# Attention block with a key and value cache: transposing key loads with rows of 16 keys in place of 4

## The chip, the cores and the metric

The kernel runs on one core of one Trainium2 chip. The metric is the device time of one launch in microseconds (us). The engines are named as in the profile: PE (matrix engine; PEld is its weight load), DVE (vector engine), ACT (scalar engine), POOL (general purpose) and SP (which here only issues DMA transfers and waits).

## The reference

The reference is a multi-head attention whose keys and values come from a cache, between an input and an output projection. Everything is bf16.

```
B, Sq, D = 8, 112, 640          H, Sk, Dh = 32, 512, 192
q = (x @ wq), split into H heads of Dh
scores = q . k_cache  * Dh**-0.5          # per batch and head: 112 x 512
p = softmax(scores)
o = p @ v_cache
out = o (heads joined) @ wo               # 8 x 112 x 640
```

The inputs are `x` (8 x 112 x 640), `k_cache` and `v_cache` (8 x 32 x 512 x 192, 50.3 MB each), `wq` (640 x 6144) and `wo` (6144 x 640).

## The kernel before

**Tiling.** The 32 heads are cut into 4 groups of 8 (`HG`, `NHG`). A unit `u` is one batch with one group of 8 heads, so there are 32 units. A turn `t` is a pair of batches, 16 in all, and a step `n` is one half unit, 4 heads, 64 in all; a turn has four steps. `place(n)` gives turn, unit, batch and half of a step.

**Order of the work.** Every piece of work is entered in a plan (`Plan.add`) with its engine, the pieces it depends on, and the function that emits it. The order on each engine is written out by hand near the end (the lists `pe`, `act`, `dve`; SP's list is filled by the load functions). Semaphore waits are worked out from the dependences. An engine works through its list in order, so a piece that waits holds up everything behind it.

**One step** is: query copies (`qc`, DVE), 16 score matmuls on PE (`scores`: L270 and L272 over 128 rows, then L282 and L284 over 64 rows in pairs), for each head a pass that scales and takes the maximum (L297, DVE) and an exp (L302, ACT) that also gives the row sum, then the reciprocal (L314) and the normalisation (L306) on DVE. One step later, PE transposes p (L322), ACT and DVE copy it out (L328), and again one step later PE multiplies with the values (L344, L355) and ACT copies the result out (L363). Between these stand pieces of the query projection for later turns (L224, copied out by L230) and of the output projection for earlier turns (L378). In ACT's list the order in a step is exp 0, exp 1, the copy L363 of two steps back, exp 2, query copies, exp 3, the copy L328 of the step before. The transposes of PE depend on L363.

**Key loads.** `load_k` (L112 to L119) reads a unit's keys with a transposing DMA on SP's queue. The source is seen as rows of 4 keys (`q=4`): 8 heads x 128 rows, each 4 x 192 = 768 elements or 1,536 B. The transposition puts each group of 128 columns of a row on the 128 partitions, so the tile `kt` is `[128, 2, 3, 1024]`: 6 groups of 128 columns, written `(a m)`, and 1,024 rows. Two neighbouring keys fill three groups: `m = 0` has the first 128 elements of the even key, `m = 2` the last 128 of the odd key, `m = 1` the remaining 64 of each. There are three such buffers (`NB = 3`); a load waits until both halves of the unit three before have had their score matmuls (`kd`). The first two units are loaded in halves of 4 heads.

**Value loads.** `load_v` (L121 to L127) reads the values without transposition; partition r holds keys 4r to 4r+3 of each head. The score columns of a head therefore come out in four blocks of 128: even and odd keys (`e`, two PSUM banks), in each `a = 0, 1`, and in a block the row r. So block `(e, a)` of p is transposed to one row per partition r, and `QJ = [0, 2, 1, 3]` names the key of the group of 4 that belongs to it.

**SP's queue** holds, from turn 2 on, for each turn: the two key loads, sometimes two `wq` loads, the two value loads, sometimes two `wo` loads. All transfers, with x at the start and the results at the end, go through it in that order.

Of the kernel before, what the change touches and what calls it, by code (L numbers as in the profile page):

```python
# [5 lines left out]
BF16 = mybir.dt.bfloat16  # L6
F32 = mybir.dt.float32
ACTF = mybir.ActivationFunctionType
# [44 lines left out]
def build_mha_kernel(nc, x, k_cache, v_cache, wq, wo, out):  # L53
    B, SQ, D = x.shape
# [9 lines left out]
    scale = float(DH) ** -0.5  # L64
    NB, NSS = 3, 3
    QJ = [0, 2, 1, 3]

    def place(n):

# [11 lines left out]
    with ExitStack() as es:  # L81
# [170 lines left out]

        def scores(n):
            t, u, b, half = place(n)
            ktb = kt[u % NB]
            xs = slice((b % 2) * SQ, (b % 2 + 1) * SQ)

            def raw(j, c):
                return qr[:, t % 2, 2 * half + j, c, xs]

            def cs(i):
                return slice((4 * half + i) * 128, (4 * half + i + 1) * 128)

            for j in range(2):
                def emit(e, j=j):
                    for h in range(2):
                        i = 2 * j + h
                        ev, od = (raw(j, 0), qh[:, n % 2, j, 1, :]) if h == 0 else (qh[:, n % 2, j, 2, :], raw(j, 2))
                        hs = slice(h * 256, (h + 1) * 256)
                        e.matmul(ps[0:SQ, 2 * j, hs], ev, ktb[:, :, 0, cs(i)], start=(h == 0), stop=False,  # L270
                                 skip_group_check=True)
                        mm = e.matmul(ps[0:SQ, 2 * j + 1, hs], od, ktb[:, :, 2, cs(i)], start=(h == 0), stop=False,  # L272
                                      skip_group_check=True)
                    return mm
                add("PE", ("Sm", n, j), [("qc", n), k_of(n), ("smax", n - 1, 2 * j), ("smax", n - 1, 2 * j + 1)], emit)
            for i in range(4):
                def emit(e, i=i):
                    j, h = divmod(i, 2)
                    ev, od = ((raw(j, 1)[0:64], qh[64:128, n % 2, j, 0, :]) if h == 0 else
                              (qh[0:64, n % 2, j, 3, :], raw(j, 1)[64:128]))  # L280
                    hs = slice(h * 256, (h + 1) * 256)
                    m1 = e.matmul(ps[0:SQ, 2 * j, hs], ev, ktb[0:64, :, 1, cs(i)], start=False, stop=True,  # L282
                                  skip_group_check=True)
                    m2 = e.matmul(ps[0:SQ, 2 * j + 1, hs], od, ktb[64:128, :, 1, cs(i)], start=False, stop=True,  # L284
                                  skip_group_check=True)
                    return m1, m2
                add("PE", ("St", n, i), [], emit, ("PE", "PE2"))

        def softmax(n):
            for i in range(4):  # L290
# [8 lines left out]
                                           op0=ALU.mult, op1=ALU.min, accum_out=nmx[:, k:k + 1])  # L299

                def exp(e, k=k, a=a):
                    return e.activation(p_sb[:, k, :], s_sb[:, a, :], ACTF.Exp, bias=nmx[:, k:k + 1], scale=-1.0,  # L302
                                        accum_out=rsum[:, k:k + 1])

                def norm(e, k=k):
# [310 lines left out]
```

## Time and profile before

| | |
|---|---|
| time, 3 runs | median 478.77 us (475.12 to 479.36) |
| profiled execution | 477.02 us, span in the profile 475.2 us |
| mean granted PE clock | 0.986 |
| busy | PE 434.7, PEld 392.8, DVE 360.9, ACT 330.3 us |
| score matmuls L270, L272, L282, L284 | 16 a step, 274 to 296 ns mean by form |
| exp L302 | 256 of 112 x 512, 712 ns mean, and 189 ns each for reading the sum |
| key loads L117 | 34 issues, 10.3 us median from issue to landing |
| value loads L125 | 30 of 1,536 KB, 10.3 us, and 4 of half the size, 6.0 us |
| DMA | 119.62 MB, 252 GB/s over the span |

An instruction's line is its line in the kernel. A mean of one instruction on PE includes its passage through the array; matmuls follow each other more closely than that. "Busy" is the time in which an engine had at least one instruction at work. Idle time of an engine that bounds nothing costs nothing. Step times quoted later run from the first score matmul of one step to that of the next.

### The profile page before, as it was taken

The numbers are of one execution on the slowest core, as the hardware profiler recorded it, in microseconds if no ns is written. First come the engines' busy times: TensorE is split into PE (matmuls) and PEld (weight loads), VectorE is DVE, ScalarE is ACT, GpSimd is POOL, SyncE is SP. The second block draws the span as 40 slices with busy tenths as digits, with TensorE's granted clock in tenths as the row PEclk, the third lists the DMA queues.
The fourth block names the chain that finished last, engine by engine and source line by source line (L and its number), as shares of the span: only waits on it lengthen the run. The fifth ranks groups of instructions, "written<-read, shape, count | busy, mean of one in ns | idle before, by whom it ended". The sixth has DMA issues, their size and how long they took to land.

```text
span 475.2 us, 14596 instructions
## 1 busy us (share of the span) xinstructions
PE 434.7 (91%) x6116; PEld 392.8 (83%) x6116; DVE 360.9 (76%) x1153; ACT 330.3 (70%) x778; POOL 0.7 (0%) x6
## 2 busy tenths in 40 slices
PE   3588669999999999999999799989989999999986
PEld 3477559999978888898999789879978989989876
DVE  0576748889878887888888688878968888888771
ACT  2376736778757775886778578767857877677673
POOL 0000000000000000000000000000000000000000
PEclk9799979999999999999999999999999999999999
DMA  8999999999999999999999999999999999999201
GB/s 184 294 269 218 311 260 239 347 217 329 282 287 249 251 324 205 329 213 310 268 225 307 221 341 195 283 265 219 326 228 342 189 295 235 315 223 321 90 17 46
DMA packets 253569, 119.62 MB, mean 252 GB/s; under 512 B 203456, under 2 KB 253504, under 8 KB 253504
## 3 DMA queue, kind: packets, MB, share of 16 engines
q1 hardware_dynamic: 253504, 118.70, 106.5%
q8 instruction: 48, 0.79, 0.7%
q14 instruction: 17, 0.14, 0.1%
HBM read 66.06 MB, written 1.15 MB: 141 GB/s over the span
## 4 chain that ended last, share of the span: by engine, by line
PE 65%; DMA 23%; SPq 6%; ACT 3%; issue 1%; DVE 1%; DVEq 0%
DMA kt<-in_k_cache_dram 18%; PE ps L378 14%; PE ps L224 12%; PE ps L355 9%; PE ps L322 8%; PE ps L282 6%; PE ps L344 5%; PE ps L270 5%; DMA vt<-in_v_cache_dram 5%; PE ps L272 4%; SPq L117 4%; ACT p_sb L302 2%; SPq L131 1%; PE ps L410 1%; ACT oT_sb L363 1%
## 5 line engine op out<-in xcount | busy, mean ns | idle before, releaser
L302 ACT ACTIVATE p_sb<-s_sb,nmx 112x512 bf16<-112x512 f32 x256 | 182.3, 712 | 117.0 <-DVE s_sb L297 117.0
L297 DVE TENSOR_SCALAR_CACHE_REDUCE s_sb<-ps 112x512 f32<-112x512 f32 x256 | 161.6, 687 | 59.1 <-PE ps L284 59.1
L224 PE MATMUL ps<-xT_sb,wq_sb 128*128 128x224 bf16 x960 | 115.4, 265 | 8.7 <-DMA wq_sb<-in_wq_dram 7.2
L378 PE MATMUL ps<-oT_sb,wo_sb 128*128 128x224 bf16 x900 | 105.0, 259 | 1.0 <-ACT oT_sb L363 1.0
L224 PEld LDWEIGHTS ps<-xT_sb,wq_sb 128*128 128x128 bf16 x960 | 91.2, 100 | 11.4 <-issue 7.2
L378 PEld LDWEIGHTS ps<-oT_sb,wo_sb 128*128 128x128 bf16 x900 | 83.7, 98 | 1.1 <-ACT oT_sb L363 1.1
L306 DVE TENSOR_SCALAR p_sb<-p_sb,rinv 112x512 bf16<-112x512 bf16 x256 | 78.9, 350 | 4.6
L230 ACT ACTIVATE qr<-ps 128x448 bf16<-128x448 f32 (+1 forms) x128 | 55.6, 439 | 16.4 <-PE ps L224 16.3
L322 PE MATMUL ps<-ident,p_sb 112*128 112x112 bf16 x1024 | 61.3, 213 | 2.8 <-ACT oT_sb L363 2.7
L322 PEld LDWEIGHTS ps<-ident,p_sb 112*128 112x128 bf16 x1024 | 53.3, 98 | 10.3 <-ACT oT_sb L363 10.3
L355 PE MATMUL ps<-pT_sb,vt 128*128 128x112 bf16 x1024 | 61.5, 213 | 0.0
L328 ACT ACTIVATE pT_sb<-ps 128x896 bf16<-128x896 bf16 x64 | 57.7, 902 | 1.6 <-PE ps L322 1.6
L355 PEld LDWEIGHTS ps<-pT_sb,vt 128*128 128x128 bf16 x1024 | 51.4, 98 | 5.0
L270 PE MATMUL ps<-kt,qr 128*112 128x256 bf16 x128 | 35.8, 279 | 20.6 <-DMA kt<-in_k_cache_dram 12.9
L328 DVE COPY pT_sb<-ps 128x896 bf16<-128x896 bf16 x64 | 40.0, 624 | 13.3 <-PE ps L322 12.9
L302 ACT ACTIVATION_READ_ACCUMULATOR p_sb<-s_sb,nmx 112x1 f32 x256 | 48.3, 189 | 0.0
L363 ACT ACTIVATE oT_sb<-ps 128x672 bf16<-128x672 f32 x64 | 45.3, 708 | 3.0 <-PE ps L355 3.0
L344 PE MATMUL ps<-pT_sb,vt 128*64 128x112 bf16 x1024 | 37.4, 216 | 3.3 <-ACT p_sb L302 1.6
L344 PEld LDWEIGHTS ps<-pT_sb,vt 128*64 128x64 bf16 x1024 | 28.1, 110 | 15.0 <-issue 11.8
L270 PEld LDWEIGHTS ps<-kt,qr 128*112 128x112 bf16 x128 | 16.8, 132 | 23.3 <-issue 10.3
L270 PE MATMUL ps<-kt,qh 128*112 128x256 bf16 x128 | 35.5, 277 | 0.0
L272 PE MATMUL ps<-kt,qh 128*112 128x256 bf16 x128 | 35.5, 277 | 0.0
(35 smaller groups left out, 424.9 us busy)
## 6 DMA issues: line engine op xcount, KB each, us to landing
vt<-in_v_cache_dram SPq DMA_DIRECT2D x30, 1536.0 KB, 10.3
wq_sb<-in_wq_dram SPq DMA_DIRECT2D x16, 480.0 KB, 5.2
wo_sb<-in_wo_dram SPq DMA_DIRECT2D x16, 480.0 KB, 12.6
vt<-in_v_cache_dram SPq DMA_DIRECT2D x4, 768.0 KB, 6.0
out_dram<-o_out SPq DMA_DIRECT2D x8, 140.0 KB, 1.9
kt<-in_k_cache_dram SPq DMA_TRANSPOSE x34, 10.3
xT_sb<-in_x_dram SPq DMA_TRANSPOSE x3, 6.2
```

The lines of the kernel that those rows point to most:

```text
L224: mm = e.matmul(ps[:, bank, j * S2:(j + 1) * S2], wq_sb[:, hg % 2, dc, c0:c0 + 128], xT_sb[:, dc, bp * S2:(bp + 1) * S2], start=(dc == 0), ...
L230: return e.activation(qr[:, t % 2, lp, blocks[0]:blocks[0] + n, :], ps[:, bank, 0:n * S2].rearrange("p (c s) -> p c s", c=n), ACTF.Copy)
L270: e.matmul(ps[0:SQ, 2 * j, hs], ev, ktb[:, :, 0, cs(i)], start=(h == 0), stop=False, skip_group_check=True)
L272: mm = e.matmul(ps[0:SQ, 2 * j + 1, hs], od, ktb[:, :, 2, cs(i)], start=(h == 0), stop=False, skip_group_check=True)
L297: return e.tensor_scalar(s_sb[:, a, :].rearrange("p (e c) -> p e c", e=2), ps[0:SQ, 2 * j:2 * j + 2, h * 256:(h + 1) * 256], -scale, None, ...
L302: return e.activation(p_sb[:, k, :], s_sb[:, a, :], ACTF.Exp, bias=nmx[:, k:k + 1], scale=-1.0, accum_out=rsum[:, k:k + 1])
L306: return e.tensor_scalar(p_sb[:, k, :], p_sb[:, k, :], rinv[:, k:k + 1], None, op0=ALU.mult)
L322: mm = e.transpose(psb[:, 4 + j, c:c + SQ], p_sb[:, (4 * n + 2 * j + h) % 8, q * 128:(q + 1) * 128], ident[0:SQ, 0:SQ])
L328: return e.activation(dst, src, ACTF.Copy) if j == 0 else e.tensor_copy(dst, src)
L344: mm = e.matmul(ps[64 * h:64 * h + 64, 4 + j, SQ:2 * SQ], vtb[:, 4 * half + 2 * j + h, d0:d0 + 64], pT(j, h, q), start=(q == 0), stop=(q = ...
L355: mm = e.matmul(ps[:, 4 + j, 2 * h * SQ:(2 * h + 1) * SQ], vtb[:, 4 * half + 2 * j + h, d0:d0 + 128], pT(j, h, q), start=(q == 0), stop=(q ...
L378: mm = e.matmul(ps[:, 7, j * S2:(j + 1) * S2], wo_sb[:, hg % 2, k, m * 128:(m + 1) * 128], oT_sb[:, t % 2, k, :], start=(k == 0), stop=(k ...
```

## The change

The source of a key load is seen as rows of 16 keys (`KQ = 16`): 8 heads x 32 rows (`KR = 32`), each 3,072 elements or 6,144 B, so 24 groups of 128 columns (`NC`). The tile `kt` has the same size but the shape `[128, 24, 256]`, with the groups written `(k a m)`: k = 0 to 3, then a and m as before. Key number 16r + 4k + 2a + e stands in row r, r = 0 to 31.

A score matmul still has 256 columns, but reads them as `a` (2), `k` (4), 32 rows: 8 runs of 32 columns, where there were 2 runs of 128. The scores of one block `(e, a)` therefore come out in the order k, r. The value rows want position 4r + k, since key 16r + 4k + 2a + e lies in value row 4r + k. The exp reads its 512 elements in the order in which they stand and writes each to that position: within a block of 128, 32 elements 4 apart, four times over. The pass that scales and takes the maximum, the normalisation, the transposes, the value matmuls, the value loads, the order of the queues and all dependences are as before.

```diff
+    KQ = 16
+    KR = SK // KQ
+    NC = KQ * DH // 128
...
-        kt = [sb(f"kt{j}", [128, 2, 3, HG * 128], BF16) for j in range(NB)]
+        kt = [sb(f"kt{j}", [128, NC, HG * KR], BF16) for j in range(NB)]
...
-                src = k_cache[b, hg * HG + lo:hg * HG + hi].rearrange("u (r q) d -> (u r) (q d)", q=4)
-                dst = kt[u % NB][:].rearrange("p a m c -> p (a m) c")[:, :, lo * 128:hi * 128]
+                src = k_cache[b, hg * HG + lo:hg * HG + hi].rearrange("u (r q) d -> (u r) (q d)", q=KQ)
+                dst = kt[u % NB][:, :, lo * KR:hi * KR]
                 return e.dma_start_transpose(dst, src)
...
-            ktb = kt[u % NB]
+            ktb = kt[u % NB][:].rearrange("p (k a m) c -> p a k m c", a=2, m=3)
...
-                return slice((4 * half + i) * 128, (4 * half + i + 1) * 128)
+                return slice((4 * half + i) * KR, (4 * half + i + 1) * KR)
...
-                        e.matmul(ps[0:SQ, 2 * j, hs], ev, ktb[:, :, 0, cs(i)], start=(h == 0), stop=False,
+                        e.matmul(ps[0:SQ, 2 * j, hs], ev, ktb[:, :, :, 0, cs(i)], start=(h == 0), stop=False,
...
-                    m1 = e.matmul(ps[0:SQ, 2 * j, hs], ev, ktb[0:64, :, 1, cs(i)], start=False, stop=True,
+                    m1 = e.matmul(ps[0:SQ, 2 * j, hs], ev, ktb[0:64, :, :, 1, cs(i)], start=False, stop=True,
...
-                    return e.activation(p_sb[:, k, :], s_sb[:, a, :], ACTF.Exp, bias=nmx[:, k:k + 1], scale=-1.0,
+                    dst = p_sb[:, k, :].rearrange("p (j r k) -> p j k r", j=4, r=KR)
+                    src = s_sb[:, a, :].rearrange("p (j k r) -> p j k r", j=4, r=KR)
+                    return e.activation(dst, src, ACTF.Exp, bias=nmx[:, k:k + 1], scale=-1.0,
                                         accum_out=rsum[:, k:k + 1])
```

The other two score matmuls (L272, L284) change in the same way.

More of the change, by code (lines that the diff above doesn't have):

```diff
@@ L269, in emit @@
                         hs = slice(h * 256, (h + 1) * 256)
[L270 removed]
+                        e.matmul(ps[0:SQ, 2 * j, hs], ev, ktb[:, :, :, 0, cs(i)], start=(h == 0), stop=False,
                                  skip_group_check=True)
[L272 removed]
+                        mm = e.matmul(ps[0:SQ, 2 * j + 1, hs], od, ktb[:, :, :, 2, cs(i)], start=(h == 0), stop=False,
                                       skip_group_check=True)
@@ L281, in emit @@
                     hs = slice(h * 256, (h + 1) * 256)
-                    m1 = e.matmul(ps[0:SQ, 2 * j, hs], ev, ktb[0:64, :, 1, cs(i)], start=False, stop=True,
+                    m1 = e.matmul(ps[0:SQ, 2 * j, hs], ev, ktb[0:64, :, :, 1, cs(i)], start=False, stop=True,
                                   skip_group_check=True)
-                    m2 = e.matmul(ps[0:SQ, 2 * j + 1, hs], od, ktb[64:128, :, 1, cs(i)], start=False, stop=True,
+                    m2 = e.matmul(ps[0:SQ, 2 * j + 1, hs], od, ktb[64:128, :, :, 1, cs(i)], start=False, stop=True,
                                   skip_group_check=True)
```

## The prediction

> **What bounds the kernel now.** I read the page's busy shares and the chain that ended last first, then how long a step takes in the stretches, then the packets of the DMA queue, then the order of instructions within one step.
>
> ```profile
> PE 434.7 (91%) x6116; PEld 392.8 (83%) x6116; DVE 360.9 (76%) x1153; ACT 330.3 (70%) x778; POOL 0.7 (0%) x6
> PE 65%; DMA 23%; SPq 6%; ACT 3%; issue 1%; DVE 1%; DVEq 0%
> ```
>
> TensorE sets most of the time and the key loads much of the rest. One turn of the loop is a pair of batches, four steps, and takes this long when nothing is late:
>
> ```profile
> 84.96:91.30 6.34, 6.34 (x94) 5.72 (x93) 5.60 (x19) 5.03 (x13) 0.00 (x0) 1.00 1.07 370
> 91.30:97.62 6.32, 6.32 (x93) 5.71 (x92) 5.58 (x19) 5.01 (x13) 0.00 (x0) 1.00 1.36 277
> 97.62:105.00 7.38, 7.38 (x105) 6.95 (x104) 5.68 (x19) 5.75 (x13) 0.00 (x0) 1.00 1.09 189
> 105.00:111.33 6.33, 6.33 (x93) 5.72 (x92) 5.82 (x19) 4.39 (x12) 0.00 (x0) 1.00 1.12 266
> ```
>
> The columns are the stretch, its length, PE, PEld, DVE, ACT, POOL, the granted clock, the DMA share and GB/s. PE is busy all the time, and the turn takes 26.37 us. From the first score matmul of step 8 (78.64 us) to that of step 60 (432.38) there are 13 turns: 353.7 us against 13 x 26.37 = 342.8. So 10.9 us of that stretch are stalls, nearly all of them steps that wait for the even batch's keys (scores of steps 16, 20, 24, 28, 36, 48 and 52 start 0.1 us after that load landed). The DMA queue is almost as long as PE's turn: stretches from one pair of key loads to the next last 25.25 to 27.75 us, so a change in the price of a key load shows at once. Within a turn:
>
> ```profile
> 125.25:130.00 4.75, 4.75 (x81) 4.49 (x76) 3.94 (x14) 3.72 (x9) 0.00 (x0) 1.00 1.27 290
> 130.00:132.00 2.00, 1.53 (x17) 1.28 (x14) 1.41 (x4) 1.40 (x4) 0.00 (x0) 1.00 0.96 104
> 132.00:136.75 4.75, 4.33 (x64) 3.91 (x64) 2.98 (x9) 1.68 (x5) 0.00 (x0) 1.00 1.27 290
> 138.00:148.50 10.50, 10.50 (x158) 9.45 (x156) 9.10 (x29) 7.88 (x20) 0.00 (x0) 1.00 1.05 371
> ```
>
> Two key loads run at 290 GB/s with a slow 2 us between them; the value and weight loads behind them run at 371.
>
> **Part 1, the key load (L115 to L117).** A transposing load is cut into packets. The page says what size:
>
> ```profile
> DMA packets 253569, 119.62 MB, mean 252 GB/s; under 512 B 203456, under 2 KB 253504, under 8 KB 253504
> kt<-in_k_cache_dram SPq DMA_TRANSPOSE x34, 10.3
> xT_sb<-in_x_dram SPq DMA_TRANSPOSE x3, 6.2
> ```
>
> All keys and x are 50.33 + 1.15 MB, which is 201,088 packets of 256 B: that is the 203,456 short ones less the few bytes that each transfer signals with. So rows of 1,536 B (keys) and of 1,280 B (x) are both read in pieces of 128 columns. The change makes a row 6,144 B; one load of eight heads goes from 1,024 rows x 6 column groups to 256 rows x 24, and both are 6,144 packets. At 290 GB/s these 1.573 MB take 5.42 us before and after. The 34 issues on SP keep their order and their waits, and nothing is moved past anything: cost **0**, which is what I take, since two row lengths gave the same packets.
>
> Bounds. From above: the price of a column group on SP. The first x load has 5 groups and its issue took 1.34 us:
>
> ```profile
> 0.74 1.34 SPq L131 DMA_TRANSPOSE xT_sb<-in_x_dram  x1
> ```
>
> At most 0.27 us a group, so 24 groups are at most 6.4 us, 1.0 more than the 5.42 of data that covers them: with cover gone, 2 loads x 13 turns x 1.0 = 26, and 4 loads' worth ahead of step 6, +30 in all. A lower price is just as open: per block of 16 rows (70 in that load) it would be 19 ns, and the count of blocks (384 a load) does not change. From below: were 6 KB rows moved like the value rows, 1.573 MB at 371 GB/s take 4.24 us, 1.18 less per load. A turn of DMA falls by 2.4 and lies under PE's 26.37, so the 10.9 us of stalls go, and at the start, where steps 4 and 6 wait for their keys, 4 x 1.18 = 4.7: **-15.6**, no more, because PE then bounds everywhere.
>
> A rule of the Trainium skill speaks against my zero. Its page "DMA: Bandwidth & Descriptors", section "Latency and other measured facts", gives DMA transposes 261 GB/s where the reads cannot be joined to at least 4 KB, and 350 to 400 where they are contiguous. Our 290 lies between; if the rule means that a 6 KB row is joined, the sum would be near that of the -15.6 case, by the row of 256 B packets it is zero.
>
> **Part 2, the score matmuls (L270, L272, L282, L284).** The 16 of a step read 256 columns as 8 runs of 32 (64 B) in place of 2 runs of 128. Rows by size:
>
> ```profile
> L355 PE MATMUL ps<-pT_sb,vt x1024: 212/213/223, 31.1 to 467.2; 128*128 128x112 bf16 x171
> L378 PE MATMUL ps<-oT_sb,wo_sb x900: 257/259/269, 68.8 to 454.2; 128*128 128x224 bf16 x180
> L270 PE MATMUL ps<-kt,qr x128: 272/273/459, 13.7 to 454.8; 128*112 128x256 bf16 x128
> ```
>
> From 112 to 224 contiguous columns the median grows by 46 ns, 0.41 a column; on that line 256 contiguous columns would be 272, and two runs took 273. A break costs 1 ns or less. Six more breaks are at most 6 ns; the pairs of L282 and L284 run side by side, so a step has 12 slots: at most 72 ns a step, 4.6 us over 64 steps, all on the path since PE is full. From below nothing: the columns stay 256. I take **0**.
>
> **Part 3, exp (L302).** It writes p with a step of 4 elements (8 B) where it wrote contiguously; it still reads contiguously, and there are still 256 exps of 512 elements. This is the part whose cover is thinnest. From the order of one step:
>
> ```profile
> 87.25 0.72 ACT L302 ACTIVATE p_sb<-s_sb,nmx 112x512 bf16<-112x512 f32 x1 [1.31 <-DVE s_sb L297]
> 87.97 0.71 ACT L302 ACTIVATE p_sb<-s_sb,nmx 112x512 bf16<-112x512 f32 x1
> 88.68 0.71 ACT L363 ACTIVATE oT_sb<-ps 128x672 bf16<-128x672 f32 x1
> 89.44 0.80 PEld L322 LDWEIGHTS ps<-ident,p_sb 112*128 112x128 bf16 x16 [0.18 <-ACT oT_sb L363]
> ```
>
> Two exps stand ahead of the eviction L363, and the transposes L322 on PE start 0.05 us after it, having waited. The page gives that wait 40 times in 64 steps (10.3 us in PEld). So ACT, at 5.0 of 6.33 us busy, is still on the path: an exp that takes d longer lengthens a step by up to 2d. The trace has no ACT write with a step between elements. Bounds: nothing, if an element keeps its slot (no gain either: the count is the same); at most a second slot each, 512 x 0.76 ns (524 less 353 ns over 224 elements, the two forms of L230) = 0.39 us, which is 0.78 x 40 = 31 to 0.78 x 64 = 50 us. I take **0**, by the rows of short runs (L363 writes runs of 112 and reads across two banks at 707 ns for 672 elements, no dearer per element than L230).
>
> The page "SBUF — State Buffer", section "Door 1: The DMA port swizzle", holds that two accesses to a 16 B line are enough for full rate, up to a step of 8 bf16; a step of 4 would be free by it, which no run here shows yet.
>
> After exp, p has the order of the value rows again (position 4r + k), so norm, transposes and value matmuls are untouched, and the maximum and the sum don't depend on the order.
>
> **Sum.** The profiled execution took 477.0 us (span 475.2 and 1.8 around it); the median shown is 478.8. 0 + 0 + 0 leaves 478.8 on that scale, with its own range 474 to 483 (the lowest run shown, 475.1, rounded down; 4.6 of matmul breaks above). About 1% is what a measurement of this kernel can tell from no change.
>
> **Rivals.**
> - *Whole rows.* The reads of a 6 KB row are joined and key loads run at the value loads' 371 GB/s. For: 290 beside 371 in one turn, same bytes. Against: 1,280 and 1,536 B rows were both cut at 256 B. 478.8 - 15.6 = **463**. Chance 0.18, and 0.02 for smaller gains over 1%: shorter slow phases in those 2 us stretches.
> - *Slow exp* (slower). Place: the two exps before L363; price 2d a step. It decides from d = 0.06 us (2 x 0.06 x 40 = 4.8 us, 1%); ACT's idle time doesn't help, as L363 is queued behind them and PE waits for that. At half a slot (0.2 us, 40 steps) **495**, at a whole one 510 to 529. For: a step between elements is new here. Against: nothing in the rows prices it. Chance 0.2.
> - *Dearer key loads* (slower). 24 groups cost SP more than the data hides, or sixteen rows 6 KB apart (96 KB a block for 24) are read more slowly; it decides from 14 ns x 16 blocks = 0.23 us a group. At the bound 478.8 + 30 = **509**; a lower read rate has no row to bound it. Chance 0.12.
> - *Breaks* in the matmuls dearer than one run break showed: over 483.6 from 75 ns a step. Chance 0.05.
> - That the change doesn't do what it says is my forecast: the rows are longer in the pattern, the packets stay 256 B. Chance 0.43.
>
> **How the numbers follow.** Faster 0.18 + 0.02 = 0.2; slower 0.2 + 0.12 + 0.05 = 0.37; the rest 0.43. The range goes down to the whole-rows case, 463, and up to 500, past the half-slot exp; left out are the full-slot exp (some 0.1), the upper part of the dearer loads (0.06) and a little below.
>
> **What would show it.** Right: 203,456 packets under 512 B again, key stretches at 290 GB/s, L302 at 711 ns, L270 at 273, turns of 26.37 us. Wrong: larger packets or over 300 GB/s in the key stretches (whole rows); L302 above 750 ns and longer waits of L322 for L363 (slow exp); key stretches under 280 GB/s or the issues of L117 (6.6 to 7.7 us where they wait for no buffer) longer by a microsecond (dearer loads); L270 above 280 ns (breaks).

## The result and the profile after

The kernel after takes 545.74 us (median of 4 runs, 542.84 to 549.11), against 477.95 (475.12 to 479.36) for the kernel before on the same chip: 1.143 times as long, with a 95% interval of 1.134 to 1.152. The prediction was 478.8 with a range of 463 to 500. Its rival "slow exp" is what happened, at a price above that rival's bound.

The lines of the code have moved: exp is now L308 (L302 before), the maximum pass L300, the eviction of the value matmuls L369 (L363), the transposes of p L328 (L322) and their copy L334 (L328), ACT's copies of the projected queries L233 (L230), the score matmuls L273, L275, L285 and L287, the key load L120 (L117).

First the busy shares and the chain that ended last:

```profile
PE 453.0 (83%) x6116; PEld 392.8 (72%) x6116; DVE 374.2 (69%) x1153; ACT 470.3 (86%) x778; POOL 0.7 (0%) x6
...
ACT 54%; PE 34%; issue 6%; DVE 4%; DMA 1%; SPq 0%; DVEq 0%
```

ACT has grown from 330.3 to 470.3 us and now holds 54% of the chain, where it held 3%. The transfers (DMA), 23% of the chain before (18% key loads, 5% value loads), are down to 1%, and PE from 65% to 34%. So ACT is now the largest part of what bounds the kernel. The groups of ACT's lines (busy us, then mean ns of one) show which instruction grew, and the table of waits (us in total, times, longest) who waits for it:

```profile
L308 ACT ACTIVATE p_sb<-s_sb,nmx 112x512 bf16<-112x512 f32 x256 | 350.7, 1428 | 52.8 <-DVE s_sb L300 52.8
L308 ACT ACTIVATION_READ_ACCUMULATOR p_sb<-s_sb,nmx 112x1 f32 x256 | 65.4, 255 | 0.0
...
L369 ACT ACTIVATE oT_sb<-ps 128x672 bf16<-128x672 f32 x64 | 48.6, 759 | 2.0 <-PE ps L361 2.0
```

```profile
DVE rinv L320 <- ACT p_sb L308: 83.7, 124, 1.8
PEld ps L328 <- ACT oT_sb L369: 69.5, 61, 2.0
```

The same rows of the kernel before:

```profile
L302 ACT ACTIVATE p_sb<-s_sb,nmx 112x512 bf16<-112x512 f32 x256 | 182.3, 712 | 117.0 <-DVE s_sb L297 117.0
L363 ACT ACTIVATE oT_sb<-ps 128x672 bf16<-128x672 f32 x64 | 45.3, 708 | 3.0 <-PE ps L355 3.0
```

```profile
PEld ps L322 <- ACT oT_sb L363: 10.3, 40, 1.3
```

One exp takes 1,428 ns, twice its 712. The same elements are computed and the same bytes are written; only the places differ. All 256 exps lie between 1,410 and 1,451 ns, whatever else ran beside them, so a collision with another engine's work is unlikely to be the cause. Reading the sum takes 255 ns (189 before), and L369, which has the same shape and the same operands as before, 759 (708). The transposes on PE wait for L369 61 times in 64 steps, 69.5 us, where it was 40 times and 10.3 us.

What the prediction called unchanged is unchanged. The page's line of packets, the row of the score matmuls by tile, and a stretch inside a key load (columns as in the prediction):

```profile
DMA packets 253569, 119.62 MB, mean 220 GB/s; under 512 B 203456, under 2 KB 253504, under 8 KB 253504
```

```profile
L273 PE MATMUL ps<-kt,qr x128: 272/273/459, 14.3 to 521.2; 128*112 128x256 bf16 x128
```

```profile
213.00:217.75 4.75, 3.73 (x57) 3.46 (x54) 3.80 (x14) 4.50 (x8) 0.00 (x0) 1.00 1.28 290
```

There are 203,456 packets under 512 B again although a row is now 6,144 B, 290 GB/s again inside a load, and 273 ns again for a score matmul that reads 8 runs.

**Where the time lies.** From the first score matmul of step 8 to that of step 60 it is 407.4 us, before 353.7: 53.7 us of the span's 69.1 (544.3 less 475.2); 6.8 more come ahead of step 8 and 8.6 behind step 60. A turn took 6.33, 6.33, 6.33 and 7.38 us plus 0.84 of waiting on average, nearly all for keys (27.21). Now it takes 7.76, 7.76, 7.76 and 8.00, together 31.28, and the mean of 13 turns is 31.34. PE's table of waits names a key load five times before (12.9 us) and not once now: the stalls for keys are gone, since the DMA queue needs 25.25 to 27.75 us a turn (the prediction's stretches). So the loss by exp is larger than the difference of times by those 10 us.

### The profile page after: what moved, and what is told of

Read it like the earlier page. It is cut to its first block, busy times and chain, and to the rows that moved or that the text cites. A ratio compares the mean times of both kernels' runs of the same rounds, so it can differ in the third digit from the quotient of the medians.

```text
span 544.3 us, 14596 instructions
## 1 busy us (share of the span) xinstructions
PE 453.0 (83%) x6116; PEld 392.8 (72%) x6116; DVE 374.2 (69%) x1153; ACT 470.3 (86%) x778; POOL 0.7 (0%) x6
## 2 busy tenths in 40 slices
DMA packets 253569, 119.62 MB, mean 220 GB/s; under 512 B 203456, under 2 KB 253504, under 8 KB 253504
## 4 chain that ended last, share of the span: by engine, by line
ACT 54%; PE 34%; issue 6%; DVE 4%; DMA 1%; SPq 0%; DVEq 0%
ACT p_sb L308 43%; PE ps L227 8%; ACT oT_sb L369 6%; PE ps L273 5%; PE ps L285 5%; PE ps L275 5%; PE ps L384 4%; DVE s_sb L300 4%; ACT qr L233 3%; PE ps L328 3%; PE ps L416 1%; DMA wq_sb<-in_wq_dram 1%; PE ps L287 1%; PE ps L361 0%; ACT pT_sb L334 0%
## 5 line engine op out<-in xcount | busy, mean ns | idle before, releaser
L308 ACT ACTIVATE p_sb<-s_sb,nmx 112x512 bf16<-112x512 f32 x256 | 350.7, 1428 | 52.8 <-DVE s_sb L300 52.8
L300 DVE TENSOR_SCALAR_CACHE_REDUCE s_sb<-ps 112x512 f32<-112x512 f32 x256 | 166.7, 688 | 34.7 <-ACT p_sb L308 18.8
L227 PE MATMUL ps<-xT_sb,wq_sb 128*128 128x224 bf16 x960 | 117.4, 268 | 21.3 <-ACT qr L233 14.0
L227 PEld LDWEIGHTS ps<-xT_sb,wq_sb 128*128 128x128 bf16 x960 | 88.8, 101 | 34.5 <-ACT qr L233 24.8
L328 PE MATMUL ps<-ident,p_sb 112*128 112x112 bf16 x1024 | 62.2, 215 | 54.3 <-ACT oT_sb L369 54.3
L328 PEld LDWEIGHTS ps<-ident,p_sb 112*128 112x128 bf16 x1024 | 52.3, 98 | 69.6 <-ACT oT_sb L369 69.5
L320 DVE RECIPROCAL rinv<-rsum 112x2 f32<-112x2 f32 x128 | 21.2, 166 | 83.7 <-ACT p_sb L308 83.7
L233 ACT ACTIVATE qr<-ps 128x448 bf16<-128x448 f32 (+1 forms) x128 | 57.6, 454 | 10.0 <-PE ps L227 10.0
L308 ACT ACTIVATION_READ_ACCUMULATOR p_sb<-s_sb,nmx 112x1 f32 x256 | 65.4, 255 | 0.0
L334 ACT ACTIVATE pT_sb<-ps 128x896 bf16<-128x896 bf16 x64 | 60.4, 944 | 2.1 <-PE ps L328 2.1
L369 ACT ACTIVATE oT_sb<-ps 128x672 bf16<-128x672 f32 x64 | 48.6, 759 | 2.0 <-PE ps L361 2.0
L334 DVE COPY pT_sb<-ps 128x896 bf16<-128x896 bf16 x64 | 39.9, 624 | 8.2 <-PE ps L328 4.9
L273 PE MATMUL ps<-kt,qr 128*112 128x256 bf16 x128 | 35.9, 281 | 7.4 <-DVE qh L251 7.4
L275 PE MATMUL ps<-kt,qh 128*112 128x256 bf16 x128 | 35.7, 279 | 0.0
L273 PE MATMUL ps<-kt,qh 128*112 128x256 bf16 x128 | 35.6, 278 | 0.0
```

Source lines behind the costliest of these rows:

```text
L227: mm = e.matmul(ps[:, bank, j * S2:(j + 1) * S2], wq_sb[:, hg % 2, dc, c0:c0 + 128], xT_sb[:, dc, bp * S2:(bp + 1) * S2], start=(dc == 0), ...
L233: return e.activation(qr[:, t % 2, lp, blocks[0]:blocks[0] + n, :], ps[:, bank, 0:n * S2].rearrange("p (c s) -> p c s", c=n), ACTF.Copy)
L273: e.matmul(ps[0:SQ, 2 * j, hs], ev, ktb[:, :, :, 0, cs(i)], start=(h == 0), stop=False, skip_group_check=True)
L300: return e.tensor_scalar(s_sb[:, a, :].rearrange("p (e c) -> p e c", e=2), ps[0:SQ, 2 * j:2 * j + 2, h * 256:(h + 1) * 256], -scale, None, ...
L308: return e.activation(dst, src, ACTF.Exp, bias=nmx[:, k:k + 1], scale=-1.0, accum_out=rsum[:, k:k + 1])
L328: mm = e.transpose(psb[:, 4 + j, c:c + SQ], p_sb[:, (4 * n + 2 * j + h) % 8, q * 128:(q + 1) * 128], ident[0:SQ, 0:SQ])
```

## The experiments

All times are medians; the ratio is to the kernel before on the same chip, with its 95% interval. Where there is no ratio, the kernel ran once, with a profile. "Step" is the time from one step's first score matmul to the next one's, the median of the same step in turns 2 to 14; three of the four steps of a turn are usually alike.

### One part at a time: e1 and e2

e1 is the kernel after with exp written as it was; e2 is the kernel before with nothing but exp's new write. In both, p's columns do not stand in the order of the value rows; each leaves that out, and the count and size of all instructions stay.

```diff
# e1, against after
-                    dst = p_sb[:, k, :].rearrange("p (j r k) -> p j k r", j=4, r=KR)
-                    src = s_sb[:, a, :].rearrange("p (j k r) -> p j k r", j=4, r=KR)
-                    return e.activation(dst, src, ACTF.Exp, bias=nmx[:, k:k + 1], scale=-1.0,
+                    return e.activation(p_sb[:, k, :], s_sb[:, a, :], ACTF.Exp, bias=nmx[:, k:k + 1], scale=-1.0,
# e2, against before
-                    return e.activation(p_sb[:, k, :], s_sb[:, a, :], ACTF.Exp, bias=nmx[:, k:k + 1], scale=-1.0,
+                    dst = p_sb[:, k, :].rearrange("p (j r k) -> p j k r", j=4, r=32)
+                    src = s_sb[:, a, :].rearrange("p (j k r) -> p j k r", j=4, r=32)
+                    return e.activation(dst, src, ACTF.Exp, bias=nmx[:, k:k + 1], scale=-1.0,
```

Expected of e1:

> The changed kernel with its long key rows and its score matmuls in runs of 32, but with exp writing contiguously as before; the reordering of p is left out, all instructions and bytes are otherwise those of the change. If exp alone carries the loss (theory 1): L302-type exps back at 711 ns and 474 to 483 us, no different from before by more than 1%. If long rows or short runs carry part of it (rival): more than 483 us, with 30 us (half the loss) at 510. If the long rows help and exp hid it: under 473.

Expected of e2:

> The kernel before with only exp's write pattern changed to a step of 4 elements; keys and score matmuls as before, so p's columns come out in another order. Theory 1: exp at 1,428 ns and 540 to 551 us, the whole loss of the change. Rival (long rows or short runs carry part): clearly below 540, 510 if they carry half.

Measured: e1 474.61 us, ratio 0.9991 (0.9963 to 1.0018); e2 544.45 us, ratio 1.1452 (1.1407 to 1.1497). The exp's group in e1:

```profile
L305 ACT ACTIVATE p_sb<-s_sb,nmx 112x512 bf16<-112x512 f32 x256 | 182.3, 713 | 114.2 <-DVE s_sb L300 114.2
```

and in e2:

```profile
L305 ACT ACTIVATE p_sb<-s_sb,nmx 112x512 bf16<-112x512 f32 x256 | 350.9, 1429 | 54.9 <-DVE s_sb L297 54.9
```

The long rows and the short runs together cost and gain nothing that could be measured (within 0.4%). Exp's write makes the whole loss: e2 has the same exp, the same steps (7.76 and 8.00) and the same mean turn (31.34) as the kernel after.

### What a written element costs: e3, e4, e5 and e12

A step has four exps, so one kernel can hold four forms of it, one for each head. All four kernels are the kernel before with other access patterns of exp; p's columns come out in other orders, and only durations are read from them. e4 and e5 change a little more: in steps 0 to 43 the exp of the fourth head writes f32 into the memory of `oF`, from where the normalisation reads it, and each exp also depends on the last normalisation of two steps back.

e3 writes bf16 contiguously, and with a step of 2, 4 and 8 elements:

```diff
+                    def form(m):
+                        return (p_sb[:, k, :].rearrange("p (j r k) -> p j k r", j=4, k=m),
+                                s_sb[:, a, :].rearrange("p (j k r) -> p j k r", j=4, k=m))
...
+                    if i == 1:
+                        return e.activation(*form(2), ACTF.Exp, **kw)
...
```

> The kernel before with four forms of exp's write, one for each head of a step: contiguous, step 2 (4 B), step 4 (8 B), step 8 (16 B); p's columns in other orders. For the mean of one exp: if the price is that of writing a 2-byte element alone (theory a), steps 2, 4 and 8 all take 1,428 ns and contiguous 711. If it grows with the bytes of a step (theory b), step 2 lies between, some 950, and step 8 above 1,428, by doubling again some 2,800. If it starts at lines of 16 B (theory c), step 2 and 4 would be 711, which step 4 has already refuted in the changed kernel, and only step 8 dearer still.

The groups of ACT in e3 (step 8; step 4; the copy of p, which follows the step of 8; step 2; contiguous):

```profile
L312 ACT ACTIVATE p_sb<-s_sb,nmx 112x512 bf16<-112x512 f32 x64 | 163.8, 2559 | 0.0
L311 ACT ACTIVATE p_sb<-s_sb,nmx 112x512 bf16<-112x512 f32 x64 | 91.9, 1435 | 0.0
L337 ACT ACTIVATE pT_sb<-ps 128x896 bf16<-128x896 bf16 x64 | 75.6, 1182 | 1.4 <-PE ps L331 1.4
L309 ACT ACTIVATE p_sb<-s_sb,nmx 112x512 bf16<-112x512 f32 x64 | 54.6, 853 | 0.0
L307 ACT ACTIVATE p_sb<-s_sb,nmx 112x512 bf16<-112x512 f32 x64 | 46.2, 723 | 43.4 <-DVE s_sb L297 43.4
```

The price is not one for "a step", and it isn't one for an element either: it grows with the step. Divide the memory into lines of 16 B and count, in the order of writing, how often the exp moves on to a line (a visit). A step of 2 puts 4 elements into one 16 B line before it goes to the next (128 visits to a line for 512 elements), a step of 4 puts 2 (256 visits), a step of 8 one (512). From 256 to 512 visits the exp grows by 1,124 ns, 4.4 ns a visit; 285 ns + 4.45 ns x visits gives 855, 1,424 and 2,563 ns against the measured 853, 1,435 and 2,559. By the same sum a contiguous exp, with 64 visits, would be 570; it took 711 to 723, so something else bounds it.

e4 asks whether it is the write or the step as such, and e5 whether the 16 B line is the unit. Their forms, in order of the heads:

```diff
# e4: read f32 with step 4; read f32 with step 32; write bf16 in pairs, 16 B between starts; write f32 with step 4
# e5: write bf16 with step 16; write bf16 in pairs, 8 B between starts; read f32 with step 2; write f32 with step 2
...
+                        return e.activation(p_sb[:, k, :].rearrange("p (r k w) -> p k r w", r=64, k=4),     # e4, third
+                                            s_sb[:, a, :].rearrange("p (k r w) -> p k r w", r=64, k=4), ACTF.Exp, **kw)
```

> The kernel before with four other forms of exp, one for each head of a step: reading float32 with a step of 4 (16 B) and writing contiguously; reading with a step of 32 (128 B) and writing contiguously; writing pairs of neighbouring bf16 with a step of 16 B between pairs; writing float32 with a step of 4 (16 B), in steps 0 to 43 only. p's columns in other orders. If the price lies on single 2-byte writes (theory a): reads 711 ns both, pairs between 711 and 1,070 ns, float32 with a step 711. If it lies on any step on the write side (theory b): pairs about 1,070, float32 with a step 1,428 or more, reads 711. If it lies on any pattern that is not one run, on either side (theory d): all four at 1,400 or more.

> The kernel before with four more forms of exp, one for each head of a step, p's columns in other orders. A rule fitted to the forms measured so far (theory f): an exp takes some 285 ns and then the longest of 0.83 ns an element, 4.45 ns for each 16 B line that it writes in 2-byte pieces apart from each other, 1.85 ns for each 16 B line that it writes in whole 4-byte words or reads. It gives: bf16 with a step of 16 (32 B, 512 lines) 2,563 ns, as the step of 8 did; pairs of bf16 with 8 B from pair to pair (128 lines, whole words) 711; reading float32 with a step of 2 (256 lines) 759; writing float32 with a step of 2 (256 lines) 759. Rival (theory b, the price grows with the bytes of a step): bf16 with a step of 16 near 4,800 ns, pairs above 711 as every second write jumps. Rival (price for each jump, whatever the width): pairs near 1,430 (256 jumps of 8 B).

ACT's groups in e4 (first, second, fourth and third form):

```profile
L306 ACT ACTIVATE p_sb<-s_sb,nmx 112x512 bf16<-112x512 f32 x64 | 79.0, 1234 | 85.3 <-DVE s_sb L299 85.3
L309 ACT ACTIVATE p_sb<-s_sb,nmx 112x512 bf16<-112x512 f32 x64 | 75.3, 1177 | 0.0
...
L316 ACT ACTIVATE oF<-s_sb,nmx 112x512 f32<-112x512 f32 x44 | 53.6, 1218 | 0.0
L312 ACT ACTIVATE p_sb<-s_sb,nmx 112x512 bf16<-112x512 f32 x64 | 48.9, 764 | 0.0
```

and in e5 (in order):

```profile
L306 ACT ACTIVATE p_sb<-s_sb,nmx 112x512 bf16<-112x512 f32 x64 | 159.4, 2490 | 97.3 <-DVE s_sb L299 97.3
...
L309 ACT ACTIVATE p_sb<-s_sb,nmx 112x512 bf16<-112x512 f32 x64 | 56.2, 878 | 0.0
...
L312 ACT ACTIVATE p_sb<-s_sb,nmx 112x512 bf16<-112x512 f32 x64 | 48.9, 764 | 0.0
...
L316 ACT ACTIVATE oF<-s_sb,nmx 112x512 f32<-112x512 f32 x44 | 33.6, 764 | 0.0
```

A step of 16 bf16 (32 B) costs no more than one of 8 (2,490 against 2,559): once every element has a 16 B line of its own, a wider step adds nothing. Steps in f32, 4 B an element, cost far less for the same number of visits: 764 ns at 256 visits and 1,218 to 1,234 at 512, some 1.8 ns a visit, and it makes little difference whether the reads or the writes have the step. Pairs of bf16, which are whole 4-byte words, cost the same 764 at 256 visits. By these rows two things set the price: how many visits to 16 B lines there are, and whether a visit brings whole 4-byte words (1.8 ns) or single 2-byte pieces (4.45 ns). This sum was fitted to the kernel after, e3 and e4; e5 tested it on four new forms, and three came within 75 ns. All pairs here start on a 4-byte boundary; whether pairs across one cost more was not run.

The fourth form missed: pairs with 8 B between starts (128 visits) took 878, not the 711 of a contiguous form. It stands behind the exp with a step of 16, though, and in e3 the copy behind the step of 8 was also slower, 1,182 ns against the 902 of the kernel before. e12 measures the pairs with no such neighbour: pairs at 8 B, contiguous, pairs at 32 B, and runs of 4 elements at 16 B.

> The kernel before with forms of exp written in short runs, after ordinary neighbours, p's columns in other orders: pairs of bf16 with 8 B from pair to pair, contiguous, pairs with 32 B from pair to pair, runs of four with 16 B. The pairs at 8 B took 878 ns behind the exp with a step of 16, whose late writes may have held them up by up to 280 ns. By the rule on 16 B lines with whole words (1.85 ns a line, 711 at least): pairs at 8 B 711, pairs at 32 B 764 as at 16 B, runs of four 711. If each jump costs something of its own: pairs at 8 B again near 870.

ACT's groups in e12 (third, first, fourth, second form):

```profile
L309 ACT ACTIVATE p_sb<-s_sb,nmx 112x512 bf16<-112x512 f32 x64 | 48.4, 756 | 0.0
L304 ACT ACTIVATE p_sb<-s_sb,nmx 112x512 bf16<-112x512 f32 x64 | 46.2, 723 | 115.7 <-DVE s_sb L297 115.7
L311 ACT ACTIVATE p_sb<-s_sb,nmx 112x512 bf16<-112x512 f32 x64 | 45.6, 713 | 0.0
...
L307 ACT ACTIVATE p_sb<-s_sb,nmx 112x512 bf16<-112x512 f32 x64 | 45.2, 706 | 0.0
```

The first exp of a step takes 723 also where it is contiguous (e3, L307), so pairs at 8 B and runs of 4 are free, pairs at 32 B cost 45 to 50 ns, and the surplus in the 878 of e5 has to come from its place behind the exp with a step of 16. The four single runs took 545.54 (e3), 519.35 (e4), 549.1 (e5) and 480.37 us (e12).

### A smaller step: e6

The whole change with rows of 8 keys (`KQ = 8`): exp writes with a step of 2.

> The whole change with rows of 8 keys (3 KB) in place of 16, so exp writes with a step of 2 elements. Exp at 853 ns, d = 0.142 us. If a step grows by 2d as in the changed kernel (6.33 to 7.76 us there): three steps of a turn 6.61 us, the fourth 7.38, a turn 27.2, about as long as the DMA queue's mean turn of 27.2, so that the stalls mostly go and what is left is 1 to 10 us: 476 to 486. If the loss went with the rows' length, halfway: 510.

Measured: 479.82 us, ratio 1.0098 (1.0062 to 1.0134). Its exps:

```profile
L308 ACT ACTIVATE p_sb<-s_sb,nmx 112x512 bf16<-112x512 f32 x256 | 217.2, 863 | 100.1 <-DVE s_sb L300 100.1
```

Exp takes 863 ns and the steps are 6.53, 6.53, 6.53 and 7.38. The exp is 0.15 us longer, the step 0.20. This also shows how little spare time there was: a fifth of the increase already costs 1%.

### From a longer exp to a longer step: e7 to e10 and e13 to e16

Below, a ring is a chain of work, each piece waiting for the one before, that leads from exp 0 of one step to exp 0 of the next; the longest ring sets the step. The prediction had a law for this: two exps stand ahead of the eviction L363, for which PE waits, so a step grows by up to twice an exp's increase. 2 x 0.716 = 1.43, and 6.33 + 1.43 = 7.76, which is the step measured. The eight kernels of this part ask whether that is the reason. None has other work than its base; they only write the order on ACT or DVE differently.

e7 is the kernel after with L369 taken between exp 0 and exp 1; e8 is the same move in the kernel before.

```diff
-            act += [("exp", n, 0), ("exp", n, 1)]
+            act += [("exp", n, 0)]
             if n > 1:
                 act += [("evPV", n - 2)]
+            act += [("exp", n, 1)]
```

> The changed kernel with one line of ACT's order moved: the copy L369 stands after the first exp of a step, not after the second. If the loss runs over the two exps ahead of that copy, on which the transposes wait (theory 1), a step loses one d (0.72 us) of its 1.43 until ACT's own sum, some 7.25 us a step, bounds: 7.76 becomes 7.25 and the time some 520 us. Rival, that ACT's sum or the wait of the reciprocals for exps 2 and 4 bounds already: no change, 540 to 548.

> The kernel before with the same one line of ACT's order moved. If the transposes' wait for that copy (0.18 us, 40 times in PEld) costs time there: up to 8 us less, 467 to 475, as far as key loads don't take it back. If PE is full anyway: 475, no change. If the later exp 1 delays the normalisation: up to 40 us more.

Measured: e7 541.12 us, ratio 1.1378 (1.1312 to 1.1444); e8 472.4 us, ratio 0.995 (0.9917 to 0.9983). In e7 only one exp is left ahead of L369, but the steps are 7.76 still. The waits of e7 say where PE stands now:

```profile
DVE rinv L320 <- ACT p_sb L308: 102.9, 124, 2.2
PEld ps L227 <- ACT qr L233: 80.1, 59, 2.7
```

The wait for L369 has left the table, and the query matmuls wait for the copy L233 in its place. So the two exps ahead of L369 can't be what alone sets the step, though the law's number fits. The kernel after shows it too: behind the wait for L369 PE waits once more, for L233 0.17 us (in the timeline below).

e9 and e10 test the next theory, that the ring closes through exp 3, the reciprocal and two norms, which stand on DVE ahead of the next maximum pass. They move those three behind that pass, e9 with the move of e7 and e10 without it.

```diff
-            dve += [("smax", n, i) for i in range(4)]
+            dve += [("smax", n, 0)]
+            if n:
+                dve += [("rc", n - 1, 1), ("norm", n - 1, 2), ("norm", n - 1, 3)]
+            dve += [("smax", n, i) for i in range(1, 4)]
...
-            dve += [("rc", n, 1), ("norm", n, 2), ("norm", n, 3)]
+            dve += [("rc", n, 1), ("norm", n, 2), ("norm", n, 3)] if n == NN - 1 else []
```

> The changed kernel with the moved copy L369 and, beside it, DVE's order changed: the reciprocal and the two normalisations of heads 3 and 4 stand after the first maximum pass of the next step. The run with the copy alone left the step at 7.76 us, with ACT waiting 0.53 us before the first exp for a maximum pass that stood behind those three on DVE. Theory 3 (a second ring, through the four exps, reciprocal, two normalisations, the next maximum pass and the next exp, is as long as the first through two exps and the transposes): with both cut, ACT's own sum of 7.25 us a step bounds, and the time is 508 to 518 us. Rival (ACT cannot be packed closer): 535 or more.

> The changed kernel with DVE's order alone changed. Theory 3: the first ring, over the two exps ahead of L369, still gives 7.76 us: no change, 538 to 548 us. Rival (the ring over DVE was the only one): the same 508 to 518 as with both.

Measured: e9 540.83 us, ratio 1.1324 (1.1251 to 1.1397), not the 508 to 518 expected; e10 553.99, ratio 1.1604 (1.1546 to 1.1661), slower than its 538 to 548. In e10 the second maximum pass comes behind the norms and exp 1 starts 1.34 us after exp 0, not 1.25; how much of the surplus this makes was not tried. In e9 PE's largest wait is still that for L233:

```profile
DVE s_sb L300 <- PE ps L287: 85.2, 63, 5.0
PEld ps L227 <- ACT qr L233: 81.4, 60, 2.9
```

So a third reading was made from the trace of the kernel after. This is one of its steps, from the timelines of ACT, PE and DVE (start us, us, engine, line; in brackets the wait before it):

```profile
307.09 1.45 ACT L308 ACTIVATE p_sb<-s_sb,nmx 112x512 bf16<-112x512 f32 x1 [0.75 <-DVE s_sb L300]
...
308.34 1.42 ACT L308 ACTIVATE p_sb<-s_sb,nmx 112x512 bf16<-112x512 f32 x1
...
309.56 0.76 ACT L369 ACTIVATE oT_sb<-ps 128x672 bf16<-128x672 f32 x1
...
310.22 1.43 ACT L308 ACTIVATE p_sb<-s_sb,nmx 112x512 bf16<-112x512 f32 x1
...
310.37 0.96 PE L328 MATMUL ps<-ident,p_sb 112*128 112x112 bf16 x16 [1.01 <-ACT oT_sb L369]
...
311.45 0.58 ACT L233 ACTIVATE qr<-ps 128x448 bf16<-128x448 f32 x1
...
312.08 0.65 PE L227 MATMUL ps<-xT_sb,wq_sb 128*128 128x224 bf16 x5 [0.17 <-ACT qr L233]
...
314.12 0.69 DVE L300 TENSOR_SCALAR_CACHE_REDUCE s_sb<-ps 112x512 f32<-112x512 f32 x1
...
314.85 1.44 ACT L308 ACTIVATE p_sb<-s_sb,nmx 112x512 bf16<-112x512 f32 x1 [0.53 <-DVE s_sb L300]
```

Exps follow each other at 1.22 to 1.25 us, although each lasts 1.43: each overlaps the next by some 0.2. Before, they came 0.71 to 0.72 apart. So an exp delays what stands behind it by 0.51 to 0.53 us more, not by 0.716. The ring that closes last goes from exp 0 over three exps and L369 to the end of L233 (307.09 to 312.03, 4.94 us), then over the query matmuls and the scores to the maximum pass (314.12) and to the next exp 0 (314.85): 7.76. In the kernel before, where exp 0 of the step shown in the prediction starts at 87.25, L230 ended 3.28 us after it, and PE came 0.29 later, without having waited for it:

```profile
90.00 0.53 ACT L230 ACTIVATE qr<-ps 128x448 bf16<-128x448 f32 x1
90.82 0.64 PE L224 MATMUL ps<-xT_sb,wq_sb 128*128 128x224 bf16 x5
```

Three exps at 0.51 to 0.53 and two copies at 0.05 make the 1.66 us more (4.94 less 3.28). Of the 0.29 some 0.05 is the hand-over itself, so 0.24 of spare time goes off: 1.42, and 1.43 was measured.

e13 opens this ring and the one over the norms together: L233 is taken ahead of exp 1 as well, with DVE's order of e9. e14 has ACT's new order alone.

```diff
             if n > 1:
                 act += [("evPV", n - 2)]
+            act += [("evQa", g) for g in q_now] + [("exp", n, 1)]
...
-            act += [("exp", n, 2)] + [("evQa", g) for g in q_now] + [("exp", n, 3)] + [("oout", b) for b in f_now]
+            act += [("exp", n, 2), ("exp", n, 3)] + [("oout", b) for b in f_now]
```

> The kernel after with three orders written differently and no other work: ACT takes the copies L369 and L233 (the 448 form) directly behind exp 0, ahead of exps 1 to 3; DVE takes the reciprocal and the norms of heads 3 and 4 behind the next step's first maximum pass. Theory 4: what sets a step after the change is not the two exps ahead of L369 but a ring of ACT, PE and DVE: exp 0, exp 1, L369, exp 2, L233 (4.94 us from the start of exp 0 to the end of L233 in the trace), the query matmuls and the scores behind L233 on PE (2.07), the maximum pass (0.75), together 7.76; a second ring through exp 3, the reciprocal and two norms is within 0.05 us of it. That is why moving L369 alone, or both L369 and the norms, left 7.76: L233 stayed behind three exps. With both rings opened, ACT's own work is left, 7.24 us a step (7.76 less its 0.52 idle): steps of 7.2 to 7.35, 16 turns shorter by 1.6 to 2.2, so 540.8 less 26 to 35 us: 505 to 516 us. Rival: ACT cannot be packed closer, since it waits for the maximum pass behind its last instruction whatever the order: 535 to 542 us.

> The kernel after with the ACT order of the run before this one and DVE's order left as it is. Theory 4: the second ring still closes, exp 3 to reciprocal to two norms to the next maximum pass to exp 0, all four exps and both copies in it: 7.7 to 7.8 us a step, 535 to 543 us. Rival: the ring through L233 alone sets the step, so that this order is enough: 505 to 520 us.

Measured: e13 539.29 us, ratio 1.1301 (1.1234 to 1.1367); e14 540.14, ratio 1.1307 (1.1227 to 1.1388). e14 lies in theory 4's interval, e13 does not: its steps are 7.71. Its waits name yet another hand-over (e14's as well, 76.9 us), so e14's time does not speak for the theory:

```profile
DVE rinv L320 <- ACT p_sb L308: 77.7, 64, 2.3
PEld ps L273 <- DVE qh L251: 76.1, 59, 5.2
```

PE's scores wait for DVE's copies of the odd queries, which stand behind a reciprocal that waits for exp 1. e15 takes these copies ahead of the reciprocal as well; e16 does so but leaves the norms of heads 3 and 4 where they were.

```diff
+            dve += [("qc", n + 1)] if n + 1 < NN and n > 1 else []
             dve += [("rc", n, 0), ("norm", n, 0), ("norm", n, 1)]
             dve += [("oacc", *o_now[0])] if two else []
-            dve += [("qc", n + 1)] if n + 1 < NN and n != 1 else []
+            dve += [("qc", n + 1)] if n == 0 else []
```

> The kernel after with the three orders of e13 and a fourth, no other work changed: DVE copies the next step's odd queries (L250, L251) before the reciprocal and the norms of heads 1 and 2, not behind them. In e13 the step was 7.71 us: exp 0, L369, L233, exp 1 (3.77 us to the end of its sum), then reciprocal, two norms and these copies on DVE (1.55), then the scores on PE that wait for the copies and the maximum pass (2.39). Theory 5: there are several rings through one or more slow exps, each within 0.1 us of 7.7; with this one opened too, every hand-over behind an exp has cover, and ACT's own length is left, 7.2 us (7.71 less its 0.52 idle): steps of 7.2 to 7.35, 13 to 16 turns shorter by 1.4 to 2.0, 507 to 521 us. Rival: ACT cannot be packed closer whatever the order, because its last instructions of a step always come before the maximum pass that it waits for: 533 to 541 us.

> As the run before this one, but DVE keeps the reciprocal and the norms of heads 3 and 4 ahead of the next step's first maximum pass. Theory 5: the ring exp 0 to 3 with both copies (6.24 us to the end of exp 3's sum in e13's trace), reciprocal and two norms (0.75), maximum pass (0.75) is 7.7 us whatever else moves: 533 to 542 us. Rival: that ring has slack, and this order is enough: 507 to 521 us.

Measured: e15 530.18 us, ratio 1.1112 (1.106 to 1.1163); e16 537.29, ratio 1.1232 (1.1174 to 1.1291). e16 is in theory 5's interval. e15 is the first order that gains anything much, about 15 us, but less than the 25 to 39 us expected. Its busy shares and its waits:

```profile
PE 437.1 (83%) x6116; PEld 398.9 (75%) x6116; DVE 359.9 (68%) x1153; ACT 476.1 (90%) x778; POOL 0.7 (0%) x6
```

```profile
PEld ps L350 <- ACT pT_sb L334: 73.1, 59, 2.3
...
ACT p_sb L308 <- DVE s_sb L300: 23.3, 22, 4.2
ACT qr L233 <- PE ps L227: 20.0, 47, 7.0
```

ACT now waits for the maximum pass in 22 steps instead of 64, and PE waits for ACT's copy L334, which stands behind three exps. A mean step is 7.60 us (30.38 a turn), and in a usual step ACT waits 0.23 of it for PE ahead of L233 and is at work nearly all the rest.

What follows: no single wait that was opened carries the loss. ACT's own work is 7.24 us a step in the kernel after (7.76 less the 0.52 in which it waits), 29.0 a turn, where PE's turn was 26.37. Beside that, the waits read as several rings of nearly the same length, each through a hand-over behind an exp: opening one shows the next (L369, L233, L251, L334). This is a reading of the traces, and no theory built on it came out in full: e7, e9, e13 and e15 were all expected to gain more than they did. Orders win back up to 15 us of the 68. The rest was not won back in any order that was run; with ACT at 7.24 a step a turn would still be 29.0 us against 27.21 before, so by an estimate from these rows some 20 us more (1.4 a turn from e15's 30.38, 13 to 16 turns) is the most that order alone could bring.

### An order for the kernel before: e11

e11 is e8 with the odd unit's value load put behind the next turn's even key load in SP's queue, to take away waits for keys.

```diff
-            for u in (2 * t, 2 * t + 1):
-                load_k(("K", u), u, 0, HG, f"mK{u % NB}", kd(u))
+            u = 2 * t
+            load_k(("K", u), u, 0, HG, f"mK{u % NB}", kd(u))
+            if t > 2:
+                load_v(("V", u - 1), u - 1, 0, HG, f"mV{(u - 1) % NB}", vd(u - 1))
+            u = 2 * t + 1
+            load_k(("K", u), u, 0, HG, f"mK{u % NB}", kd(u))
...
-            for u in (2 * t, 2 * t + 1):
+            for u in (2 * t, 2 * t + 1)[:1 if t < NT - 1 else 2]:
                 load_v(("V", u), u, 0, HG, f"mV{u % NB}", vd(u))
```

> The kernel before with the moved copy (472.4 us by itself) and SP's queue in another order from turn 2 on: the odd batch's value load of a turn is issued after the even batch's key load of the next turn, so that this key load, on which the steps stall, starts 4.1 us earlier; the value load has 10 to 14 us to spare. If the stalls of the even key loads cost what the steps show (some 11 us): 462 to 467. If they only move to the next load in the queue: 470 to 474.

Measured: 473.86 us, ratio 0.9916 (0.9889 to 0.9943). The steps without a stall are 6.23, but the mean turn is 27.00, against 26.81 in e8, because the stalls moved: PE waits for values five times, 8.2 us in all, beside three waits for keys of 9.0. Both e8 and e11 are a little faster than the kernel before, by 0.5% and 0.8%, and nothing of the change is in them.

## Why the prediction was wrong

**What bounds the kernel: right.** PE's full turn, the stalls for keys, and ACT still on the path through its copies. e6 and e8 show the last: 0.15 us more in an exp made a step 0.20 us longer, and taking one exp from ahead of L363 made it 0.10 us shorter (6.23).

**Part 1, the key load at 0: right.** 203,456 short packets and 290 GB/s, as the list of signs had it, and e1 at 0.9991. The shortest issues of a full load last 5.9 to 6.2 us, before 6.3 to 6.6, so the price of 24 column groups (+30) is out too. Beside the case of -15.6 the prediction had set the Trainium skill's page "DMA: Bandwidth & Descriptors", section "Latency and other measured facts", which gives DMA transposes 261 GB/s where the reads cannot be joined to 4 KB and about 350 to 400 where they are contiguous. Here rows of 6 KB, contiguous in memory, moved at the same 290 as rows of 1.5 KB. This case doesn't show whether the page means another kind of contiguity.

**Part 2, the short runs at 0: right.** 273 ns for 8 runs of 32 columns, and e1, at the time of the kernel before, has these matmuls too.

**Part 3, exp's write at 0: wrong. This is the step that failed**, by the term "at most a second slot each", 512 x 0.76 ns = 0.39 us. The increase was 0.716 us, 1.8 times that upper bound, and the value taken was the lower one. The bound priced an element with a step as one more element of the ordinary kind. But the cost is not per element: e3 to e5 and e12 show it per 16 B line visited, 4.45 ns where the visit writes single 2-byte pieces, and a step of 4 makes 256 visits in place of 64. The row that the text leant on, L363's runs of 112 contiguous elements, was far from this: in e12 runs of 4 elements, and even pairs, are nearly free, so a row with long runs says nothing about a write of single 2-byte elements. The text itself said that the trace had no ACT write with a step, and this should have left the upper end open.

The rule cited there, from the page "SBUF — State Buffer", section "Door 1: The DMA port swizzle", holds that two accesses to a 16 B line are enough, up to a step of 8 bf16. The measurement decides against it for ACT's writes of bf16: 853 ns at a step of 2, which has four elements to a line, 1,435 at 4 with two, 2,559 at 8 with one, against 711.

**The law of 2d: right in size by luck, wrong in reason.** It gives 1.43 us a step for d = 0.716, and 1.43 was measured in three steps of four. But an exp delays its successor by 0.52, not 0.716, and the ring held three exps and two copies; e7 took one exp out of the way of L369 and gained nothing in the step. The two errors cancelled. The law was stated for steps that waited for L363, 40 of 64; in fact 61 waited.

**The rivals.** "Slow exp" was the rival that came true, with its place (ACT ahead of what PE waits for) and its sign (L302 above 750 ns, longer waits of L322 for L363) as written. Its price stopped at 510 to 529 us because of the bound. With the measured d and the prediction's own law it would have said 478.8 + 57 to 92 us, 536 to 570, which holds the result. The stalls for keys, which the text counted as 10.9 us, vanish into the longer turn; the rival did not take them off.

## What to carry to other kernels

When a change moves a reordering into an engine's write, price the write by the 16 B lines that it visits and by whether each visit carries whole 4-byte words, not by its elements; on ACT a pair of bf16 at a time was nearly free here, and single elements 8 B apart doubled the instruction. If the profile has no row with the new access pattern, the upper bound is open, and where 0.06 us more in each exp already costs 1%, as the prediction worked out, an open bound can't be valued at 0. A law that gives the right number isn't thereby the mechanism: move the instruction that it names and see whether the time moves.

## What the runs showed that was not expected

A slow write seems to reach into the next instruction. Behind an exp with a step of 4 the read of the sum takes 255 ns instead of 189 and L369 759 instead of 708; behind one with a step of 8 the read takes 495 and the copy of p 1,182 instead of 902, some 280 ns more. So an instruction whose own work didn't change can be longer in the profile.

A step in the reads costs ACT about as much as one in f32 writes: 764 ns at 8 B, 1,234 at 16 B, and 1,177 at 128 B, against 711.

What makes the slow 2 us between two key loads (104 GB/s in the prediction's rows) was not tried and stays open.
